# Top-k lists joined by more selection rounds, token numbers looked up in DRAM, and two operations moved to other engines

## The chip, the cores and the metric

The kernel runs on one core of a Trainium2 chip. The metric is device time in microseconds (us) of one execution. Five engines work in parallel: TensorE (PE in the profile) multiplies matrices, VectorE (DVE), ScalarE (ACT) and GpSimd (POOL) work on elements, SyncE (SP) issues transfers. Each takes its instructions strictly in order, and waits for the others by semaphores.

## What is computed

Attention over 8 batches, 12 heads, 448 tokens and head size 64, with q and k normalised by their root mean square; its output, as 3584 rows of 768, goes into a layer of 8 experts in which each expert takes at most 80 tokens, those with the largest gate weight:

```python
q_n, k_n = (rmsnorm(q, g_q), rmsnorm(k, g_k))
scores = scale * np.matmul(q_n, k_n.transpose(0, 1, 3, 2))
attn = softmax(scores)
x = np.matmul(attn, v)        # as rows of tokens: (3584, 768)
logits = x @ w_gate
expert_idx = np.argmax(logits, axis=1)
gate_w = softmax(logits)[np.arange(N), expert_idx]
for e in range(8):
    tok_idx = np.where(expert_idx == e)[0]
    if len(tok_idx) > 80:
        keep = np.argpartition(-gate_w[tok_idx], 80)[:80]
        tok_idx = tok_idx[keep]
    h = np.maximum(x[tok_idx] @ w1[e], 0.0)
    out[tok_idx] = gate_w[tok_idx, None] * (h @ w2[e])
```

## The kernel before, in words

The main loop (L447) runs n from -4 to 51. It is a software pipeline written out by hand: `ctx.enter_context(tc.manual_schedule())` makes every engine take the instructions in the order in which the loop writes them. Iteration n holds steps of several pairs of heads; there are 48 pairs, six to a batch. On TensorE an iteration computes the scores of pair n (L218), the product with v of pair n-1 (`av`, L228), the transposes of q and k of pair n+1 (L203), the gate sums of pairs n-3 and n-2 if n is odd (`zl`, L256 and L260), and the transposes that bring pair n-2 out (`xout`, L418). ScalarE squares q and k (L174), copies the transposed q and k out of PSUM (L208, L210), takes the exponential of the scores (L222) and copies `xout`'s result (L421). VectorE sums the exponentials over four tiles (`presum`, L237 to L239), sums the squares (`ssq`, L180), copies the product `po` out of PSUM (`uevac`, L244) and normalises q (L195, a = 0). GpSimd makes 1/sqrt of the mean square (L183, and the power at L186) and normalises k (L195, a = 1). `po` is a single PSUM buffer, so the product of the next pair waits for its copy. The buffers of tag `tp` in PSUM, two of them, serve every transpose.

When a batch's six pairs are through, `gate1`, `gate1t`, `gate1v` and `gate2` turn its sums into gate weights `S`, zero where an expert was not chosen, and `gate3` transposes them so that experts lie along partitions (`R`). Then comes the choice of the best 80. `rounds` takes them eight at a time: the eight largest values (MAX8), their positions (FIND_INDEX8) and a replacement of these by -2 (MATCH_REPLACE8), ten times. Batches 0 to 3 are done together, as 128 partitions of 448 columns; batches 4 to 6 one by one, as 128 partitions of 112 (each batch as four lists); batch 7 after the loop, 8 partitions of 448. `merge` joins two sorted lists with a bitonic network of eight stages: three comparisons on VectorE for the values, four operations on GpSimd that move the token numbers along. `bg` holds ten such merges in all. This work stands in `queue`; `work` takes pieces from it twice in an iteration, one piece while `slow` and three otherwise.

After the loop the rest of the queue runs, then the rounds of batch 7, a last join, and two transposes that give `idxT` (token numbers) and `gwT` (weights). Eight experts follow: a gather of 80 rows by indirect DMA (L544), two matrix products, a scatter into the output (L599). Weights of experts 0 to 3 are loaded during attention by GpSimd's queue, those of 4 to 7 are rewritten as bf16 in DRAM and loaded after the loop (L134).

Of the kernel before, what the change touches and what calls it, by code (L numbers as in the profile page):

```python
# [14 lines left out]
U32 = mybir.dt.uint32  # L15
PSUM = bass.MemoryType.PSUM
# [3 lines left out]
def kernel(  # L20
# [13 lines left out]
    nc = tc.nc  # L34
# [23 lines left out]

    cpool = ctx.enter_context(tc.tile_pool(name="const", bufs=1))
# [32 lines left out]


    LW = 128
    tpool = ctx.enter_context(tc.tile_pool(name="topk", bufs=1))
    lst = tpool.tile([128, 2, LW], F32, name="lst")
    other = tpool.tile([128, 2, LW], F32, name="other")
    ping = tpool.tile([128, 2, LW], F32, name="ping")
    pong = tpool.tile([128, 2, LW], F32, name="pong")
    best = tpool.tile([128, 2, LW], F32, name="best")  # L100
    for t in (lst, other):
        nc.gpsimd.memset(t[:, 0, :], -1.0)
        nc.gpsimd.memset(t[:, 1, :], 0.0)
# [41 lines left out]
    with tc.tile_pool(name="qk", bufs=3) as qkpool, \  # L145
# [148 lines left out]
        def gate2(b):  # L294
# [16 lines left out]

            if b < 4:
                if b == 0:
                    gst[0]["S"] = gpool.tile([ST, NT, 128], F32, tag="sc4", name="sc4", bufs=1)
                    nc.gpsimd.memset(gst[0]["S"][:], 0.0)
                dst = gst[0]["S"][:, :, 32 * b:32 * b + E]
            elif b < B - 1:
                gst[b]["S"] = gpool.tile([ST, NT, 32], F32, tag="sc1", name="sc1", bufs=1)
                nc.gpsimd.memset(gst[b]["S"][:], 0.0)
                dst = gst[b]["S"][:, :, 0:E]  # L320
            else:
                gst[b]["S"] = gpool.tile([ST, NT, E], F32, tag="sc7", name="sc7", bufs=1)
                dst = gst[b]["S"][:]
            nc.vector.tensor_mul(dst, eq[:], gw[:].unsqueeze(2).to_broadcast([ST, NT, E]))

        def gate3(b):

            if b < 3:
                return
            sp = tpps.tile([128, 512], F32, tag="tp", name="sp")  # L330
            if 3 < b < B - 1:
                nc.tensor.transpose(sp[:, :ST], gst[b]["S"][:].rearrange("p j c -> p (j c)"),
                                    ident[:ST, :ST])
                R = tpool.tile([128, ST], F32, tag="R1", name="R1")
                nc.vector.tensor_copy(R[:, :], sp[:, :ST])
            else:
                src = gst[0 if b == 3 else b]["S"]
                rows = src.shape[2]
                for j in range(NT):
                    nc.tensor.transpose(sp[:rows, j * ST:(j + 1) * ST], src[:, j, :],  # L340
                                        ident[:ST, :ST])
                R = tpool.tile([rows, S], F32, tag=f"R{rows}", name="R4")
                nc.vector.tensor_copy(R[:, :].rearrange("e (p j) -> e j p", j=NT),
                                      sp[:rows, :S].rearrange("e (j p) -> e j p", j=NT))
            gst[b]["R"] = R

        def rounds(b, step, off):

            rows = E if b == B - 1 else 128
            todo = []  # L350
            idx = tpool.tile([128, CAP], U32, tag="idx", name="idx", bufs=2)

            def one(kon):
                R = gst[b]["R"]
                mv = lst[:rows, 0, kon:kon + 8]
                nc.vector.max(out=mv, in_=R[:, :])
                nc.vector.max_index(out=idx[:rows, kon:kon + 8], in_max=mv, in_values=R[:, :])
                if kon + 8 < CAP:
                    nc.vector.match_replace(out=R[:, :], in_to_replace=mv,
                                            in_values=R[:, :], imm_value=-2.0)  # L360

            for kon in range(0, CAP, 8):
                todo.append(lambda kon=kon: one(kon))
            eng = nc.vector if b == B - 1 else nc.gpsimd
            last = todo[-1]

            def fin():
                last()
                eng.tensor_scalar(lst[:rows, 1, :CAP], idx[:rows, :], float(step),
                                  offq[:rows, off:off + 1], op0=ALU.mult, op1=ALU.add)  # L370
            todo[-1] = fin
            return todo

        def merge(a, pairs, res):


            todo = []

            def first():
                for dq, src, sq in pairs:  # L380
                    nc.gpsimd.tensor_copy(other[32 * dq:32 * dq + E, :, LW - CAP:],
                                          src[32 * sq:32 * sq + E, :, CAP - 1::-1])
                m = tpool.tile([128, LW], F32, tag="m0", name="m0")
                d = tpool.tile([128, LW], F32, tag="d0", name="d0")
                nc.vector.tensor_tensor(m[:, :], other[:, 0, :], a[:, 0, :], op=ALU.is_gt)
                nc.vector.tensor_tensor(ping[:, 0, :], other[:, 0, :], a[:, 0, :], op=ALU.max)
                nc.gpsimd.tensor_sub(d[:, :], other[:, 1, :], a[:, 1, :])
                nc.gpsimd.tensor_mul(d[:, :], d[:, :], m[:, :])
                nc.gpsimd.tensor_add(ping[:, 1, :], a[:, 1, :], d[:, :])

            def stage(i):
                w = LW >> (i + 1)
                x = (ping, pong)[i % 2]
                y = res if w == 1 else (pong, ping)[i % 2]

                def half(t, c, k):
                    return t[:, c, :].rearrange("p (g two w) -> p two g w", two=2, w=w)[:, k]
                m = tpool.tile([128, LW // w // 2, w], F32, tag="m1", name="m1", bufs=2)
                d = tpool.tile([128, LW // w // 2, w], F32, tag="d1", name="d1", bufs=2)
                va, vb, ua, ub = half(x, 0, 0), half(x, 0, 1), half(x, 1, 0), half(x, 1, 1)  # L400
                nc.vector.tensor_tensor(m[:], vb, va, op=ALU.is_gt)  # L401
                nc.vector.tensor_tensor(half(y, 0, 0), vb, va, op=ALU.max)
                nc.vector.tensor_tensor(half(y, 0, 1), vb, va, op=ALU.min)
                nc.gpsimd.tensor_sub(d[:], ub, ua)
                nc.gpsimd.tensor_mul(d[:], d[:], m[:])  # L405
                nc.gpsimd.tensor_add(half(y, 1, 0), ua, d[:])
                nc.gpsimd.tensor_sub(half(y, 1, 1), ub, d[:])

            todo.append(first)
            for i in range(7):  # L410
                todo.append(lambda i=i: stage(i))
            return todo
# [14 lines left out]
        def ok(n):  # L427
# [4 lines left out]
        bg[3] = (rounds(3, 1, 0)  # L432
                 + merge(lst, [(0, lst, 1), (2, lst, 3)], best)
                 + merge(best, [(0, best, 2)], best))
        for b in range(4, B - 1):
            bg[b] = (rounds(b, NT, 1 + b)
                     + merge(lst, [(0, lst, 1), (2, lst, 3)], lst)
                     + merge(lst, [(0, lst, 2)], lst)
                     + merge(best, [(0, lst, 0)], best))
        queue = []  # L440

        def work(k):
            for _ in range(k):
                if queue:
                    queue.pop(0)()

        for n in range(-4, NP + 4):  # L447
# [14 lines left out]
            for b in range(B):  # L462
# [3 lines left out]
                if n == b * HP + HP - 1 + 4 and b < B - 1:  # L466
# [11 lines left out]
            slow = len(queue) > 0 and n < 32  # L478
            work(1 if slow else 3)
# [11 lines left out]
            if ok(n + 3):  # L491
                rstd(n + 3)
# [4 lines left out]
            work(1 if slow else 3)  # L497
# [141 lines left out]
```

## Time and profile before

| | |
|---|---|
| median of 3 runs | 666.72 us (666.6 to 666.8) |
| the profiled execution, own time | 665.04 us |
| its span, first to last instruction | 663.1 us |
| mean granted clock of TensorE | 0.893 |
| busy: TensorE, VectorE, ScalarE, GpSimd | 514.8, 469.5, 300.7, 402.8 us |

Busy times are sums over one engine and run beside each other. Stretches with different limits follow one another, so the shares of the whole span say little; the rows further down are taken by stretch. An instruction in the trace stands with its start, its duration, its line, what it writes and reads, and in brackets the idle time of its engine just before it with what ended that.

### The profile page before, as it was taken

The numbers are of one execution on the slowest core, as the hardware profiler recorded it, in microseconds if no ns is written. First come the engines' busy times: TensorE is split into PE (matmuls) and PEld (weight loads), VectorE is DVE, ScalarE is ACT, GpSimd is POOL, SyncE is SP. The second block draws the span as 40 slices with busy tenths as digits, with TensorE's granted clock in tenths as the row PEclk, the third lists the DMA queues.
The fourth block names the chain that finished last, engine by engine and source line by source line (L and its number), as shares of the span: only waits on it lengthen the run. The fifth ranks groups of instructions, "written<-read, shape, count | busy, mean of one in ns | idle before, by whom it ended". The sixth has DMA issues, their size and how long they took to land. (4 is left out here: it accounts for less than half of the span.)

```text
span 663.1 us, 9227 instructions
## 1 busy us (share of the span) xinstructions
PE 514.8 (78%) x3101; PEld 221.4 (33%) x3101; DVE 469.5 (71%) x942; ACT 300.7 (45%) x409; POOL 402.8 (61%) x594
## 2 busy tenths in 40 slices
PE   0799999999999999998767976768867775000976
PEld 0334444434434334433222322222222321000854
DVE  1586677768778777999857875669756786786432
ACT  2667667666676676665433632343434330000111
POOL 2985445555544554452799696996997928843351
PEclk9999999999999999999888986887778797555989
DMA  3365969869788697794811834426416061541862
GB/s 98 115 137 151 249 151 261 172 179 240 176 237 177 189 254 155 230 199 142 175 49 58 161 92 93 101 70 132 117 28 125 14 125 28 209 173 30 297 235 60
DMA packets 82574, 97.55 MB, mean 147 GB/s; under 512 B 9056, under 2 KB 71008, under 8 KB 81504
## 3 DMA queue, kind: packets, MB, share of 16 engines
q1 hardware_dynamic: 66912, 67.85, 33.1%
q0 software_dynamic: 15616, 29.13, 24.8%
q8 instruction: 24, 0.39, 0.2%
q14 instruction: 22, 0.18, 0.1%
HBM read 97.97 MB, written 36.74 MB: 203 GB/s over the span
## 5 line engine op out<-in xcount | busy, mean ns | idle before, releaser
L228 PE MATMUL po<-at,vt 112*64 112x448 f32 x768 | 181.2, 597 | 45.0 <-DVE us L244 45.0
L222 ACT ACTIVATE at<-ps 112x896 f32<-112x896 f32 x192 | 165.9, 915 | 48.1 <-PE ps L218 42.3
L218 PE MATMUL ps<-qkT 64*112 64x448 f32 x768 | 176.5, 580 | 2.3 <-ACT qkT L210 1.3
L186 POOL TENSOR_TENSOR rs<-ms,nhalf 112x16 f32<-112x16 f32 x48 | 141.1, 2941 | 4.0
L183 POOL TENSOR_SCALAR ms<-ssq 112x16 f32<-112x16 f32 x48 | 11.4, 238 | 152.8 <-DVE ssq L180 151.7
L228 PEld LDWEIGHTS po<-at,vt 112*64 112x64 f32 x768 | 49.6, 144 | 162.1 <-issue 87.1
L218 PEld LDWEIGHTS ps<-qkT 64*112 64x112 f32 x768 | 62.9, 178 | 60.1 <-issue 37.1
L203 PE MATMUL tp<-ident,qn 112*128 112x112 f32 x384 | 52.9, 282 | 35.8 <-DVE qn L195 18.9
L238 DVE TENSOR_TENSOR t<-at 112x896 f32<-112x896 f32 x48 | 70.6, 1471 | 0.0
L203 PEld LDWEIGHTS tp<-ident,qn 112*128 112x128 f32 x384 | 40.6, 150 | 76.1 <-issue 35.7
L180 DVE TENSOR_REDUCE ssq<-sq 112x16 f32<-112x1024 f32 x48 | 58.1, 1210 | 9.6 <-ACT sq L174 9.6
L174 ACT ACTIVATE sq<-qk 112x1024 f32<-112x1024 f32 x48 | 50.6, 1055 | 30.3 <-DVE ssq L180 21.8
L208 ACT ACTIVATE qkT<-tp,gqk 128x448 f32<-128x448 f32 x48 | 30.2, 630 | 71.8 <-PE tp L203 71.5
L244 DVE COPY us<-po 128x448 f32<-128x448 f32 x48 | 29.6, 617 | 46.1 <-PE po L228 46.1
L195 POOL TENSOR_TENSOR qn<-qk,rs 112x512 f32<-112x512 f32 x48 | 58.7, 1224 | 2.1
L421 ACT COPY xb<-xp 112x512 f32<-112x512 f32 x48 | 28.2, 587 | 66.1 <-PE xp L418 66.1
L239 DVE TENSOR_TENSOR sm<-sm,t 112x896 f32<-112x896 f32 x48 | 54.1, 1126 | 1.6
L237 DVE TENSOR_TENSOR sm<-at 112x896 f32<-112x896 f32 x48 | 53.3, 1110 | 0.0
L195 DVE TENSOR_TENSOR qn<-qk,rs 112x512 f32<-112x512 f32 x48 | 37.8, 787 | 11.7 <-POOL rs L186 11.7
L580 ACT ACTIVATE h_sb<-ph 128x320 bf16<-128x320 f32 x16 | 7.0, 437 | 76.5 <-PE ph L576 76.5
L405 POOL TENSOR_TENSOR d<-d,m 128x64 f32<-128x64 f32 x77 | 32.5, 422 | 14.3 <-DVE m L401 8.5
L401 DVE TENSOR_TENSOR m<-ping 128x64 f32<-128x64 f32 x44 | 12.0, 272 | 35.2 <-POOL d L405 34.2
(114 smaller groups left out, 587.9 us busy)
## 6 DMA issues: line engine op xcount, KB each, us to landing
w_sb<-in_moe_w_dram POOLq DMA_DIRECT2D x8, 1536.0 KB, 15.6
wb_scratch<-in_moe_w_dram POOLq DMA_DIRECT2D x8, 1536.0 KB, 11.8
w_sb<-wb_scratch SPq DMA_DIRECT2D x8, 1536.0 KB, 11.6
qk<-in_q_dram SPq DMA_DIRECT2D x48, 224.0 KB, 4.3
qk<-in_k_dram SPq DMA_DIRECT2D x48, 224.0 KB, 4.5
vt<-in_v_dram SPq DMA_DIRECT2D x48, 224.0 KB, 4.7
xr_scratch<-xb SPq DMA_DIRECT2D x48, 224.0 KB, 3.4
out_dram<-zeros SPq DMA_DIRECT2D x28, 384.0 KB, 6.6
```

The lines of the kernel that those rows point to most:

```text
L174: nc.scalar.activation(sq[:, :], st[n]["qk"][:].rearrange("p a h x -> p (a h x)"), AF.Square)
L180: nc.vector.reduce_sum(out=ssq[:, :], in_=st[n]["sq"][:].rearrange("p (g d) -> p g d", d=D), axis=AX.X)
L186: nc.gpsimd.tensor_tensor(rs[:].rearrange("p a h j -> p (a h j)"), ms[:, :], nhalf[:, :], op=ALU.pow)
L195: eng.tensor_mul(qn[:, a].rearrange("p j h d -> p h j d"), qk[:, a].rearrange("p h (j d) -> p h j d", d=D), rs[:, a].unsqueeze(3).to_broad ...
L203: nc.tensor.transpose(tp[:, j * ST:(j + 1) * ST], st[n]["qn"][:, a, j].rearrange("p h d -> p (h d)"), ident[:ST, :ST])
L218: nc.tensor.matmul(ps[:, hh, :S], st[n]["T1"][hh * D:(hh + 1) * D, j * ST:(j + 1) * ST], st[n]["T0"][hh * D:(hh + 1) * D, :], start=True, ...
L222: nc.scalar.activation(st[n]["at%d" % (j // 2)][:, j % 2], ps[:, :, :S], AF.Exp)
L228: nc.tensor.matmul(st[n]["po"][hh * D:(hh + 1) * D, :S], st[n]["v"][:, hh, j * D:(j + 1) * D], st[n]["at%d" % (j // 2)][:, j % 2, hh, :], ...
L237: nc.vector.tensor_add(sm[:], a0[:, 0], a0[:, 1])
L238: nc.vector.tensor_add(t1[:], a1[:, 0], a1[:, 1])
L239: nc.vector.tensor_add(sm[:], sm[:], t1[:])
L405: nc.gpsimd.tensor_mul(d[:], d[:], m[:])
```

## The change

There are no merges any more. The 80 best of batches 0 to 3 are taken as before; then `lists` adds each batch's first token number to the positions, stores these token numbers in a DRAM table `tab_scratch` (four transfers on SP's queue) and copies the four lists of values side by side into one row of 320 columns per expert (`cand["a"]`, GpSimd). Ten further rounds over these 320 columns give the best 80 of the four batches. Batches 4 and 5 are treated together in the same way (64 partitions of 448 columns), and joined with the 80 so far in ten rounds over 240 columns; batch 6 is written beside the 80 so far and joined in ten rounds over 528. Each of these joins ends in positions, not in token numbers. `numbers` turns positions into addresses of the table (`place`: GpSimd adds, TensorE transposes, VectorE casts), fetches the numbers with eight indirect DMAs on GpSimd's queue, one for each expert, 80 words each, and stores them for the next level (SP). Batch 7 is joined after the loop as before, with three transposes.

`work` now spends a budget of 4.2 (in us as the code reckons them) once, at an iteration's end, instead of counting pieces. `uevac` copies on ScalarE; both halves of `normalise` are on GpSimd; `rstd` stands behind `uevac`. The work of the queue is spread as follows: rounds of batches 0 to 3 in iterations 27 to 30, their join in 30 to 33, lookups in 33 and 34; rounds of batches 4 and 5 in 39 to 42, the join in 42 to 44, lookups in 45; the join with batch 6 in 46 to 50, lookups in 51.

```diff
+    LT = CAP + S
+    tab_dram = nc.dram_tensor("tab_scratch", (E, 3, LT), U32, kind="Internal").ap()
...
-            eng = (nc.vector, nc.gpsimd)[a]
-            eng.tensor_mul(
+            nc.gpsimd.tensor_mul(
...
-            nc.vector.tensor_copy(us[:, :], st[n]["po"][:, :S])
+            nc.scalar.copy(us[:, :], st[n]["po"][:, :S])
...
+            first, rows = {3: (0, 128), 5: (4, 64)}.get(b, (b, E))
...
+        def rounds(get, rows, width, val):
+            idx = tpool.tile([rows, CAP], U32, tag="idx", name="idx", bufs=2)
+            def one(kon):
+                R, v = get(), val[:, kon:kon + 8]
+                nc.vector.max(out=v, in_=R)
+                nc.vector.max_index(out=idx[:, kon:kon + 8], in_max=v, in_values=R)
                 if kon + 8 < CAP:
+                    nc.vector.match_replace(out=R, in_to_replace=v, in_values=R, imm_value=-2.0)
+            cost = (3 * (width + 60) / 960 + 0.3, )
+            return [cost + (lambda kon=kon: one(kon), ) for kon in range(0, CAP, 8)], idx
+        def lists(b0, nb, val, idx, lev, dst, col):
+            def go():
+                num = tpool.tile([32 * nb, CAP], U32, tag="num", name="num")
+                nc.gpsimd.tensor_scalar(num[:, :], idx[:, :],
+                                        offq[:32 * nb, b0 // 4:b0 // 4 + 1], None, op0=ALU.add)
+                for g in range(nb):
+                    nc.sync.dma_start(out=tab_dram[:, lev, col + g * CAP:col + (g + 1) * CAP],
+                                      in_=num[32 * g:32 * g + E, :])
+                    nc.gpsimd.tensor_copy(dst[:, col + g * CAP:col + (g + 1) * CAP],
+                                          val[32 * g:32 * g + E, :])
+            return [(0.0, go)]
+        def numbers(idx, lev, res):
+            add = tpool.tile([CAP, E], U32, tag="add", name="add")
+            def place():
+                pf = tpool.tile([E, CAP], F32, tag="pf", name="pf")
+                nc.gpsimd.tensor_scalar(pf[:, :], idx[:, :], tabF[:, :], float(lev * LT),
+                                        op0=ALU.add, op1=ALU.add)
+                tp = tpps.tile([128, 512], F32, tag="tp", name="tpn")
+                nc.tensor.transpose(tp[:CAP, :E], pf[:, :], ident[:E, :E])
+                nc.vector.tensor_copy(add[:, :], tp[:CAP, :E])
+            def fetch(e):
+                nc.gpsimd.indirect_dma_start(
+                    out=res[:, e:e + 1], out_offset=None,
+                    in_=tab_dram.rearrange("e l (s o) -> (e l s) o", o=1),
+                    in_offset=bass.IndirectOffsetOnAxis(ap=add[:, e:e + 1], axis=0))
+            def store():
+                if lev < 2:
+                    nc.sync.dma_start(out=tab_dram[:, lev + 1, :CAP].rearrange("e s -> s e"),
+                                      in_=res[:, :])
+            return ([(0.3, place)] + [(0.5, lambda e=e: fetch(e)) for e in range(E)]
+                    + [(0.0, store)])
-        def merge(a, pairs, res):
...
+        r, i = rounds(lambda: gst[3]["R"], 128, S, v03)
+        bg[3] = r + lists(0, 4, v03, i, 0, cand["a"], 0)
+        r, i = rounds(lambda: cand["a"][:, :], E, 4 * CAP, cand["b"])
+        bg[3] += r + numbers(i, 0, num3)
+        r, i = rounds(lambda: gst[5]["R"], 64, S, v45)
+        bg[5] = r + lists(4, 2, v45, i, 1, cand["b"], CAP)
+        r, i = rounds(lambda: cand["b"][:, :], E, 3 * CAP, cand["c"])
+        bg[5] += r + numbers(i, 1, num5)
+        r, i = rounds(lambda: cand["c"][:, :], E, LT, best)
+        bg[6] = r + numbers(i, 2, num6)
...
+        def work(us):
+            while queue and us > 0:
+                cost, f = queue.pop(0)
+                f()
+                us -= cost
...
-            slow = len(queue) > 0 and n < 32
-            work(1 if slow else 3)
...
-            work(1 if slow else 3)
...
+            work(4.2)
```

What the order of instructions becomes shows best in three places. The first is VectorE in an iteration that takes rounds over batches 0 to 3; before, from one `us` copy to the next (`R_2413` holds the gate weights, `lst` the lists):

```order
L244 COPY us<-po 128x448 [waits PE_49]
L356 MAX lst<-R_2413 128x8 [waits DVE_49]
L357 MAX_INDEX idx<-lst,R_2413 128x8 [waits DVE_49]
L359 MATCH_REPLACE R_2413<-lst,R_2413 128x448 [waits DVE_49]
L237 TENSOR_TENSOR sm<-at 112x896
L238 TENSOR_TENSOR t_2524<-at 112x896 [waits Activation_49]
L239 TENSOR_TENSOR sm<-sm,t_2524 112x896 [waits DVE_49]
L356 MAX lst<-R_2413 128x8
L357 MAX_INDEX idx<-lst,R_2413 128x8 [waits DVE_49]
L359 MATCH_REPLACE R_2413<-lst,R_2413 128x448 [waits DVE_49]
L195 TENSOR_TENSOR qn<-qk,rs 112x2x4x64 [waits DMAHW3_49,Pool_49]
L180 TENSOR_REDUCE ssq<-sq 112x16 [waits Activation_49]
```

And VectorE with the change at the end of iteration 30 and the start of 31, where the last round over single batches stands before the first over the joined row:

```order
L187 TENSOR_REDUCE ssq<-sq 112x16 [waits Activation_49,Pool_49]
L349 MAX v_154<-R 128x8
L350 MAX_INDEX idx<-v_154,R 128x8 [waits DVE_49]
L349 MAX candb<-canda 8x8 [waits Pool_49]
L350 MAX_INDEX idx<-candb,canda 8x8 [waits DVE_49]
L352 MATCH_REPLACE canda<-candb,canda 8x320 [waits DVE_49]
L349 MAX candb<-canda 8x8 [waits DVE_49]
L350 MAX_INDEX idx<-candb,canda 8x8 [waits DVE_49]
L352 MATCH_REPLACE canda<-candb,canda 8x320 [waits DVE_49]
L243 TENSOR_TENSOR sm<-at 112x896 [waits PE_49]
L244 TENSOR_TENSOR t_2781<-at 112x896 [waits Activation_49]
```

The copy of `po` and one `qn` are gone from VectorE, all rounds of an iteration stand behind `ssq`, and the first round over `canda` waits for GpSimd. The second place is GpSimd in iterations 33 and 34 with the change (lines L190 to L201 are the old L183 to L195, `num_157` the token numbers):

```order
L201 TENSOR_TENSOR qn<-qk,rs 112x2x4x64 [waits DMAHW2_49,PE_49,Pool_49]
L201 TENSOR_TENSOR qn<-qk,rs 112x2x4x64 [waits DMAHW3_49]
L190 TENSOR_SCALAR ms<-ssq 112x16 [waits DVE_49]
L193 TENSOR_TENSOR rs<-ms,nhalf 112x16 [waits Pool_49]
L376 TENSOR_SCALAR pf<-idx,tabF 8x80 [waits DVE_49]
L383 DMA num_157<-tab_scratch,add 80x1 [waits DMAHW1_49,DMAHW6_49,DMAHW0_49,DMAHW7_49,DMASW3_49,DVE_49]
L383 DMA num_157<-tab_scratch,add 80x1 [waits DMASW4_49]
L201 TENSOR_TENSOR qn<-qk,rs 112x2x4x64 [waits DMAHW7_49,PE_49,Pool_49]
L201 TENSOR_TENSOR qn<-qk,rs 112x2x4x64 [waits DMAHW0_49]
L190 TENSOR_SCALAR ms<-ssq 112x16 [waits DVE_49]
L193 TENSOR_TENSOR rs<-ms,nhalf 112x16 [waits Pool_49]
L383 DMA num_157<-tab_scratch,add 80x1 [waits DMASW5_49]
```

Two lookups stand ahead of the `qn` of iteration 34, and six more behind its power. The third place is TensorE at the end of iteration 33, with the change:

```order
L234 MATMUL po<-at,vt 64x448 x4
L399 MATMUL xp<-ident,us 112x128 [waits Activation_49]
L399 MATMUL xp<-ident,us 112x128 x3
L379 MATMUL tpn<-ident,pf 80x8 [waits Activation_49,Pool_49]
L224 MATMUL ps<-qkT 112x448 [waits Activation_49]
```

The transpose of `pf` stands ahead of the scores of the next iteration, and waits for GpSimd, which waits for the last round on VectorE.

## Rows read from the trace of the kernel before

**Rows 1.** The page's slices: busy tenths of TensorE and its granted clock

```profile
PE   0799999999999999998767976768867775000976
PEclk9999999999999999999888986887778797555989
```

**Rows 2.** Busy us (and instructions) of each engine by stretch, clock, DMA share, GB/s

```profile
core 0: us, PE busy (x) PEld busy (x) DVE busy (x) ACT busy (x) POOL busy (x), PEclk, DMA share, GB/s
100.00:120.00 20.00, 20.00 (x118) 7.93 (x116) 15.64 (x16) 13.69 (x19) 13.49 (x10) 1.00 0.80 218
...
400.00:420.00 20.00, 11.99 (x57) 4.82 (x57) 13.85 (x38) 7.14 (x10) 13.96 (x32) 0.79 0.62 126
...
580.00:600.00 20.00, 0.00 (x0) 0.00 (x0) 16.76 (x47) 0.00 (x0) 7.09 (x22) 0.50 0.35 149
```

**Rows 3.** TensorE in order of time: the first scores of four iterations

```profile
99.45 1.76 PE L218 MATMUL ps<-qkT 64*112 64x448 f32 x8
...
109.28 1.76 PE L218 MATMUL ps<-qkT 64*112 64x448 f32 x8
...
117.47 1.76 PE L218 MATMUL ps<-qkT 64*112 64x448 f32 x8
...
273.15 1.76 PE L218 MATMUL ps<-qkT 64*112 64x448 f32 x8
```

**Rows 4.** TensorE in order of time: a wait for VectorE's copy

```profile
327.80 3.26 PE L228 MATMUL po<-at,vt 112*64 112x448 f32 x8 [3.91 <-DVE us L244]
```

**Rows 5.** VectorE in order of time: first and last of batch 7, addresses

```profile
584.69 0.61 DVE L356 MAX8 lst<-R 8x8 f32<-8x448 f32 x1
...
604.75 0.25 DVE L369 TENSOR_SCALAR lst<-idx,offq 8x80 f32<-8x80 uint32 x1
...
606.73 0.16 DVE L536 CAST idxT<-ft 80x8 uint32<-80x8 f32 x1 [0.46 <-PE ft L533]
```

**Rows 6.** VectorE in order of time: the adds of `presum`, and `ssq`

```profile
37.42 1.08 DVE L237 TENSOR_TENSOR sm<-at 112x896 f32<-112x896 f32 x1
...
40.55 2.24 DVE L195 TENSOR_TENSOR qn<-qk,rs 112x512 f32<-112x512 f32 x1
...
302.56 1.21 DVE L180 TENSOR_REDUCE ssq<-sq 112x16 f32<-112x1024 f32 x1
303.69 0.61 DVE L244 COPY us<-po 128x448 f32<-128x448 f32 x1
```

**Rows 7.** VectorE in order of time: one round over 112 columns

```profile
541.55 0.27 DVE L356 MAX8 lst<-R 128x8 f32<-128x112 f32 x1
...
542.61 0.28 DVE L356 MAX8 lst<-R 128x8 f32<-128x112 f32 x1
```

**Rows 8.** GpSimd in order of time: root mean square and `qn`, list copies

```profile
303.86 0.21 POOL L183 TENSOR_SCALAR ms<-ssq 112x16 f32<-112x16 f32 x1 [5.88 <-DVE ssq L180]
304.15 2.90 POOL L186 TENSOR_TENSOR rs<-ms,nhalf 112x16 f32<-112x16 f32 x1
307.12 1.06 POOL L195 TENSOR_TENSOR qn<-qk,rs 112x512 f32<-112x512 f32 x1
...
546.31 0.66 POOL L381 COPY other<-lst 8x160 f32<-8x160 f32 x2
```

**Rows 9.** VectorE in order of time: a gate, from its first operation to the next `presum`

```profile
316.22 0.44 DVE L280 RECIPROCAL rz<-zt 112x48 f32<-112x48 f32 x1
...
319.81 1.08 DVE L237 TENSOR_TENSOR sm<-at 112x896 f32<-112x896 f32 x1
```

**Rows 10.** Groups of instructions and DMA issues: gathers, small pieces, us to landing

```profile
L544 POOL DMA_INDIRECT xg<-xr_scratch,idxT x8 | 8.3, 1036 | 21.4 <-issue 19.5 <-POOL xg L543 1.9
...
xr_scratch<-rz SPq DMA_DIRECT2D x8, 21.0 KB, 7.5
```

**Rows 11.** VectorE in order of time: an add beside GpSimd's normalisation

```profile
118.54 2.82 DVE L238 TENSOR_TENSOR t<-at 112x896 f32<-112x896 f32 x1
```

**Rows 12.** Instructions on `R`: duration ns min/median/max, first and last start us

```profile
L356 DVE MAX8 lst<-R x50: 260/278/621, 267.6 to 603.4; 128x8 f32<-128x112 f32 x30, 128x8 f32<-128x448 f32 x10, 8x8 f32<-8x448 f32 x10
...
L343 DVE COPY R<-sp x2: 927/938/948, 263.7 to 578.5; 128x448 f32<-128x448 f32 x1, 8x448 f32<-8x448 f32 x1
```

More of the change, by code (lines that the diff above doesn't have):

```diff
@@ L324, in gate2 @@
[L324 to L344, printed above, removed]
+            first, rows = (0, 128) if b < 4 else (4, 64) if b < 6 else (b, E)
@@ new lines, in gate2, with gate3 @@
+            if b == first:
+                gst[b]["S"] = gpool.tile([ST, NT, rows], F32, tag=f"sc{rows}", name="sc", bufs=1)
+                if rows > E:
+                    nc.gpsimd.memset(gst[b]["S"][:], 0.0)
+            r0 = 32 * (b - first)
+            nc.vector.tensor_mul(gst[first]["S"][:, :, r0:r0 + E], eq[:],
+                                 gw[:].unsqueeze(2).to_broadcast([ST, NT, E]))
+        def gate3(b):
+            if b not in (3, 5, 6, 7):
+                return
+            first, rows = {3: (0, 128), 5: (4, 64)}.get(b, (b, E))
+            sp = tpps.tile([128, 512], F32, tag="tp", name="sp")
+            for j in range(NT):
+                nc.tensor.transpose(sp[:rows, j * ST:(j + 1) * ST], gst[first]["S"][:, j, :],
+                                    ident[:ST, :ST])
+            if b == 6:
+                R = cand["c"][:, CAP:]
+            else:
+                R = tpool.tile([rows, S], F32, tag=f"R{rows}", name="R")[:, :]
+            nc.vector.tensor_copy(R.rearrange("e (p j) -> e j p", j=NT),
+                                  sp[:rows, :S].rearrange("e (j p) -> e j p", j=NT))
@@ L358, in one @@
                 if kon + 8 < CAP:
[L359 to L370, printed above, removed]
@@ L371, in rounds @@
-            todo[-1] = fin
-            return todo
-        def merge(a, pairs, res):
[L377 to L412, printed above, removed]
@@ L431 @@
         bg = {}
[L432 to L439, printed above, removed]
-        queue = []
[L442 to L445, printed above, removed]
+        v03 = tpool.tile([128, CAP], F32, name="v03")
+        v45 = tpool.tile([64, CAP], F32, name="v45")
+        best = tpool.tile([E, CAP], F32, name="best")
+        num3 = tpool.tile([CAP, E], U32, name="num3")
+        num5 = tpool.tile([CAP, E], U32, name="num5")
+        num6 = tpool.tile([CAP, E], U32, name="num6")
+        r, i = rounds(lambda: gst[3]["R"], 128, S, v03)
[8 more added lines that the diff above has]
+        bg[6] = r + numbers(i, 2, num6)
+        queue = []
+        def work(us):
[3 more added lines that the diff above has]
+                us -= cost
         for n in range(-4, NP + 4):
@@ L504 @@
                     gate3(b)
+            work(4.2)
+        while queue:
+            work(1)
     wlate = ctx.enter_context(tc.tile_pool(name="moe_w2", bufs=1))
@@ L511 @@
         fetch_late(e)
-    while queue:
-        work(1)
-    for f in rounds(B - 1, 1, B):
-        f()
-    fin = tpool.tile([E, 2, CAP], F32, name="fin")
-    fm = tpool.tile([E, CAP], F32, name="fm")
-    fd = tpool.tile([E, CAP], F32, name="fd")
-    A, Z = best[:E, :, :CAP], lst[:E, :, CAP - 1::-1]
-    nc.vector.tensor_tensor(fm[:, :], Z[:, 0], A[:, 0], op=ALU.is_gt)
-    nc.vector.tensor_sub(fd[:, :], Z[:, 1], A[:, 1])
-    nc.vector.tensor_mul(fd[:, :], fd[:, :], fm[:, :])
-    nc.vector.tensor_tensor(fin[:, 0], Z[:, 0], A[:, 0], op=ALU.max)
@@ L536 @@
-    nc.vector.tensor_copy(idxT[:, :], ft[:CAP, E:2 * E])
-    nc.vector.tensor_copy(gwT[:, :], ft[:CAP, 0:E])
+    v7 = tpool.tile([E, CAP], F32, name="v7")
+    last, lidx = rounds(lambda: gst[B - 1]["R"], E, S, v7)
+    for cost, f in last:
+        f()
+    fin = tpool.tile([E, 3, CAP], F32, name="fin")
+    nc.vector.tensor_tensor(fin[:, 0], v7[:, ::-1], best[:, :], op=ALU.is_gt)
+    nc.vector.tensor_tensor(fin[:, 1], v7[:, ::-1], best[:, :], op=ALU.max)
+    nc.vector.tensor_scalar(fin[:, 2], lidx[:, ::-1], float((B - 1) * S), None, op0=ALU.add)
@@ new lines @@
+    ft = tpps.tile([128, 512], F32, tag="tp", name="ft")
+    for i in range(3):
+        nc.tensor.transpose(ft[:CAP, i * E:(i + 1) * E], fin[:, i], ident[:E, :E])
+    old = tpool.tile([CAP, E], F32, name="old")
+    new = tpool.tile([CAP, E], F32, name="new")
+    gwT = tpool.tile([CAP, E], F32, name="gwT")
+    bad = tpool.tile([CAP, E], F32, name="bad")
+    idxT = tpool.tile([CAP, E], U32, name="idxT")
+    nc.vector.tensor_copy(old[:, :], num6[:, :])
+    nc.vector.tensor_sub(new[:, :], ft[:CAP, 2 * E:3 * E], old[:, :])
```

65 lines of the change are left out of this document (22 added, 43 removed).

## The prediction

> **What bounds the kernel now.** I read the slices of the page first, then the busy times by stretch, then each engine in order of time. Two slice rows [rows 1] give the shape: TensorE is full for 17 slices of 16.6 us, then falls to 6 to 8 tenths for most of the next sixteen, to nothing for three, and fills again for the experts; its granted clock follows it down. From 400 to 420 us TensorE works 12.0 us of 20 at a mean clock of 0.79, and VectorE and GpSimd 14 us each; from 580 to 600 TensorE does nothing, VectorE 16.8 us [rows 2]. So three stages have three limits.
>
> In the first, TensorE sets the pace: an odd iteration (with the `zl` matmuls) takes 109.28 - 99.45 = 9.83 us, the even one behind it 8.19 [rows 3]. Iteration 28 starts at 273.15, so iteration 27, where list work starts, at T = 273.15 - 9.83 = 263.3. From there TensorE waits for the `us` copy on VectorE, which stands in VectorE's queue behind list work: at 327.8 it waits 3.91 us, and the eight matmuls behind that take 3.26 us where eight of the same size take about 1.7 in [rows 3], which is the lower clock level [rows 4]. Merge stages on VectorE in turn wait for GpSimd's half. The last stage is ten rounds of batch 7 from 584.69 to 604.75 and some arithmetic; addresses are ready at 606.89, and the span ends at 663.1 [rows 5]. Those last 56.3 us are the experts, which the change does not touch.
>
> **What VectorE pays per iteration.** The three adds of `presum` take 40.55 - 37.42 = 3.13 us when nothing disturbs them, and `ssq` 303.69 - 302.56 = 1.13 [rows 6]. The `us` copy and `qn` leave, so 4.26 us stay. A round over 448 columns costs 2.07 (20.06 for ten, the last without its replace [rows 5]), one over 112 columns 542.61 - 541.55 = 1.06 [rows 7], though it has 128 partitions and the other eight: width counts. On that line 240 columns cost 1.44, 320 cost 1.69 and 528 cost 2.31.
>
> **Removed and moved.** Ten merges of eight stages leave VectorE and GpSimd, and with them the wait of TensorE for `us`: ScalarE now copies `po`. ScalarE is busy 13.7 us of 20 in the first stage [rows 2], 6.2 per 9 us iteration; a copy like VectorE's at some 0.6 fits, and I cost it at nothing. Its cover is gone only where ScalarE waits in `gate2` for VectorE, an instant that the VectorE sum below holds already. GpSimd does both `qn`: `ms`, pow and one `qn` take 307.12 - 303.86 + 1.06 = 4.3 us [rows 8], two 5.4, under 8.19. `transp` reads them more than an iteration later, so only the start pays, one `qn` or **1 us**.
>
> **First lists, iterations 27 to 33.** I follow VectorE from the end of `ssq` in iteration 27, T + 6 (some 5 us after the scores start, and 1 for adds that meet a `qn`). `work(4.2)` takes three rounds of 448 in each of 27 to 29: 6.2, then twice 4.26 + 6.2, to T + 33.1. In 30 comes the tenth round, and the next `MAX` waits for GpSimd's copies, which stand behind `ms` and pow: 3.3 us after `ssq`, then five small operations at 0.33 [rows 8], 5.0 in all; with two rounds of 320 (3.4) and 4.26 it is 12.7. Iteration 31 has the `zsb` copy (0.55) and three rounds, 9.9; iteration 32 a gate, 319.81 - 316.22 = 3.6 us [rows 9], and three rounds, 12.9; iteration 33 two rounds and `place`, which goes to GpSimd, TensorE and back (four short operations, 0.9), 8.5. That ends at T + 77.1. TensorE's own work in these seven is 4 x 9.83 + 3 x 8.19 + 0.6 for `zt` = 64.5. Its transpose in `place` must wait for VectorE, so **12.6 us** are lost there at the latest, and I add 3 for a spell at the lower clock [rows 4]. Iterations 34 to 38 have no rounds; TensorE paces them, 45.2 us with a `zt` and an `sp`. Iteration 39 starts at T' = T + 125.3.
>
> **Second and third lists, 39 to 51.** The same from T' + 6: 6.2 and twice 10.46, to T' + 33.1; iteration 42 is 4.26 + 4.3 for the wait and two rounds of 240, 11.5; 43 is 10.6; 44 has a gate, the copy into the candidates (0.95 [rows 12]) and four rounds, 14.6; 45 is 3.3. That is T' + 73.1, which TensorE's 64.9 lie inside. Iterations 46 to 48 are 3.13 + 2 x 2.31 each, 49 is 5.2, 50 is 9.1 (gate, copy of batch 7, last two rounds), `place` 0.9: T' + 111.6. Ten rounds of 448 and the closing arithmetic, about the 606.89 - 584.69 = 22.2 of today [rows 5], end at T' + 133.8; experts to **T' + 190.1**.
>
> **Lookups.** An indirect DMA holds GpSimd 1.04 us [rows 10], so eight after the first lists are 8.3 us. They delay the next `qn`, which has some 11 us before `transp` needs it; the eight at the end run beside batch 7's 20 us. I cost them at nothing at 1.04 each. The other bound is that each holds GpSimd until its words land: 7.5 us, as the small pieces of `rz` take [rows 10]; the row for an indirect DMA is the nearer one, the bound is rival (d). SP's six list stores and two stores of looked-up numbers wait ahead of later loads. Those run an iteration ahead, so I take zero, and 5 us as the upper end at each of three waits.
>
> **Sum.** 263.3 + 1.0 + 125.3 + 190.1 = 579.7 us of span. Around the span of the profiled execution lie 665.04 - 663.1 = 1.9, and the median of the runs is 1.7 above that execution: **583 us**.
>
> **The port, row against rule.** Beside GpSimd's `qn` an add of `presum` took 2.82 us [rows 11], against 1.08 undisturbed [rows 6]; no `MAX8` takes over 0.621 [rows 12]. In iterations with rounds the two `qn` begin 3.3 us after `ssq`, under the rounds, so I charge nothing beyond the 1 us above. The Trainium skill (SBUF — State Buffer, Who interferes with whom) says that a VectorE instruction with two SBUF inputs and a GpSimd instruction that reads SBUF shut each other out for a whole instruction, and that one with a single input does not contend. By that rule, the rows agree; it speaks against moving `qn`, and is the first rival.
>
> **Rivals.** (a) The moved `qn` falls on the adds after all. Then each of 13 iterations that VectorE paces and that still have a `qn` costs 2.82 - 1.08 = 1.7 more, 22 us: 605. For it: rows 11; against: the order above. (b) VectorE's lag is absorbed by buffers and TensorE alone paces: iterations 27 to 47 are 192.6 us, two short ones 7, gate and copy of batch 7 some 5, then the 22.2 and 56.3 of above; with 263.3 + 1 + 3.6 that is 551. Against: `place` puts TensorE behind VectorE twice. (c) Small costs add up: SP's waits hold back q and k, TensorE drops to the lower level more often; 15 to 25 us, around 603. (d) Slower than before: each lookup holds GpSimd until it lands. With a hold of h, the first eight cost 8h less 11.5 of cover, the second 8h less 39 (until the third lists need GpSimd), the third 8h less 22. At 1.0 + 7.5 that is 24 x 8.5 - 72.5 = 131, so 714 us; from h = 6.5 on it eats the whole gain of 84. Against: 1.04 in the row. (e) The wait removed was not the limit and another takes its place: near 665.
>
> **How the numbers follow.** Forecast (569 to 595) 0.62, (a) 0.14, (b) 0.08, (c) 0.11, (d) 0.03, (e) 0.02. The range 564 to 614 takes in the forecast, (a) and (c) with the SP waits, 0.87 nominally; I leave the rest for terms that no row shows. A measurement of this kernel tells 0.2% (1.3 us) from no change; faster by more 0.95, same 0.01, slower 0.04.
>
> **What would show it.** Right: TensorE full until the first lists, then waiting at the transpose of `place` and at `zt`, never for `us` on VectorE; iteration 39 near 390 us; batch 7's ten rounds beginning near 501; no merge groups; experts still 56 us. Wrong: `presum` adds that take over 3.5 us together where rounds run (a), GpSimd standing between lookups (d), long waits of `sq` for q or k (c).

## The result, and the profile after

The changed kernel takes **595.18 us** (median of four runs, 594.05 to 595.29) against 666.66 us (666.27 to 666.8) on the same chip: a ratio of 0.8925, 95% interval 0.8909 to 0.894. That is 71.5 us less; the forecast was 84 less, 583 us, and its range (564 to 614) holds the result. It lies at the upper edge of the forecast's own band (569 to 595), in the part of the range that was left for rivals and SP's waits. The profiled execution has a span of 593.3 us.

The slices of its page, TensorE and its granted clock, answer to [rows 1]:

```profile
PE   0699999999999999999987699399997995005795
PEclk9999999999999999999997979699997998556998
```

A slice is 14.8 us here. The long stretch of 6 to 8 tenths is gone. What is left of it are a dip around 320 us, a hole from 370 to 385 (the 3), and two empty slices ahead of the experts where there were three of 16.6 us. The groups of instructions show the moves (busy us, mean ns of one, then idle time just before them):

```profile
L234 PE MATMUL po<-at,vt 112*64 112x448 f32 x768 | 168.2, 560 | 0.1
...
L201 POOL TENSOR_TENSOR qn<-qk,rs 112x512 f32<-112x512 f32 x96 | 112.2, 1196 | 2.7
...
L181 ACT ACTIVATE sq<-qk 112x1024 f32<-112x1024 f32 x48 | 50.7, 1057 | 27.2 <-DMA qk<-in_k_dram 24.6 <-DVE ssq L187 2.6
...
L383 POOL DMA_INDIRECT num<-tab_scratch,add x24 | 26.9, 1121 | 8.9 <-issue 5.7 <-DVE add L380 2.6 <-DMA w_sb<-wb_scratch 0.3
...
L250 ACT COPY us<-po 128x448 f32<-128x448 f32 x48 | 25.7, 534 | 25.4 <-PE po L234 24.7 <-issue 0.7
```

The matmuls into `po` no longer wait for the `us` copy (0.1 us in all; at one place alone it was 3.91 [rows 4]). A copy on ScalarE costs 0.53, a lookup about 1.1. What has grown is on `sq`: ScalarE waits 24.6 us for `k` from DRAM, 11.58 of them at once. Before it was 7.3, beside longer waits for `ssq`:

```profile
L174 ACT ACTIVATE sq<-qk 112x1024 f32<-112x1024 f32 x48 | 50.6, 1055 | 30.3 <-DVE ssq L180 21.8 <-DMA qk<-in_k_dram 7.3 <-DVE sm L239 1.2
```

TensorE in order of time, its long waits from iteration 27 to the experts:

```profile
314.46 1.07 PE L278 MATMUL zt<-ident,zsb 128*112 128x128 f32 x4 [4.24 <-ACT xb L402]
...
341.86 0.23 PE L379 MATMUL tpn<-ident,pf 8*80 8x8 f32 x1 [5.88 <-POOL pf L376]
342.02 3.33 PE L224 MATMUL ps<-qkT 64*112 64x448 f32 x8
...
379.80 1.10 PE L399 MATMUL xp<-ident,us 128*112 128x128 f32 x4 [8.77 <-ACT qkT L214]
...
401.87 1.76 PE L224 MATMUL ps<-qkT 64*112 64x448 f32 x8
...
451.34 1.07 PE L278 MATMUL zt<-ident,zsb 128*112 128x128 f32 x4 [3.17 <-ACT xb L402]
...
506.26 0.91 PE L333 MATMUL sp<-ident,sc 112*8 112x112 f32 x4 [7.31 <-DVE sc L323]
...
512.59 0.23 PE L379 MATMUL tpn<-ident,pf 8*80 8x8 f32 x1 [5.42 <-POOL pf L376]
...
533.33 0.40 PE L515 MATMUL ft<-ident,fin 8*80 8x8 f32 x3 [20.50 <-DVE fin L511]
```

All but one are where the prediction put them: at `zt`, at the transpose of `place`, at `sp` behind the gate of iteration 50, which its sum has on VectorE, and in the last rounds. The one that it lacks is the largest before the last batch: 8.77 us at 379.80, for `qkT`. Iteration 39 starts at 401.87; the forecast is T' = 389.6, so 12.3 us of the shortfall lie before it. What stands behind that wait is read on three engines. ScalarE:

```profile
378.17 1.06 ACT L181 ACTIVATE sq<-qk 112x1024 f32<-112x1024 f32 x1 [11.58 <-DMA qk<-in_k_dram]
379.13 0.62 ACT L214 ACTIVATE qkT<-tp,gqk 128x448 f32<-128x448 f32 x1
```

`sq` waits 11.58 us for `k`, and the `qkT` copy for TensorE stands behind it. SP's queue of DMA issues:

```profile
353.64 0.56 SPq L403 DMA_DIRECT2D xr_scratch<-xb  x1
361.35 0.31 SPq L390 DMA_DIRECT2D tab_scratch<-num  x1
361.76 0.46 SPq L166 DMA_DIRECT2D qk<-in_q_dram  x1
362.27 0.68 SPq L168 DMA_DIRECT2D qk<-in_k_dram  x1
```

The loads of `q` and `k` stand behind the store of token numbers, which waits for the lookups; those run on GpSimd from 342.57 to 359.9 and have a weight rewrite right behind them:

```profile
358.98 0.90 POOL L383 DMA_INDIRECT num<-tab_scratch,add  x1 [0.30 <-issue]
359.89 0.96 POOL L136 DMA_DIRECT2D wb_scratch<-in_moe_w_dram  x1
```

So three things meet at 360 us: loads that SP holds back, a store of 640 single words ahead of them (2.5 KB, 16.1 us from issue to landing), and 1.5 MB from DRAM to DRAM beside them:

```profile
tab_scratch<-num SPq DMA_DIRECT2D x1, 2.5 KB, 16.1
```

The experiments take these apart.

### The profile page after: what moved, and what is told of

Same layout as the page of the kernel before. It is cut to its first block, busy times and chain, and to the rows that moved or that the text cites. A ratio compares the mean times of both kernels' runs of the same rounds, so it can differ in the third digit from the quotient of the medians.

```text
span 593.3 us, 8594 instructions
## 1 busy us (share of the span) xinstructions
PE 496.1 (84%) x3110; PEld 217.9 (37%) x3110; DVE 379.5 (64%) x644; ACT 322.3 (54%) x457; POOL 354.4 (60%) x285
## 2 busy tenths in 40 slices
DMA packets 84761, 97.55 MB, mean 164 GB/s; under 512 B 11240, under 2 KB 73200, under 8 KB 83696
## 5 line engine op out<-in xcount | busy, mean ns | idle before, releaser
L234 PE MATMUL po<-at,vt 112*64 112x448 f32 x768 | 168.2, 560 | 0.1
L190 POOL TENSOR_SCALAR ms<-ssq 112x16 f32<-112x16 f32 x48 | 26.8, 557 | 150.7 <-DVE ssq L187 149.8
L201 POOL TENSOR_TENSOR qn<-qk,rs 112x512 f32<-112x512 f32 x96 | 112.2, 1196 | 2.7
L244 DVE TENSOR_TENSOR t<-at 112x896 f32<-112x896 f32 x48 | 53.0, 1105 | 30.4 <-ACT at L228 30.3
L209 PE MATMUL tp<-ident,qn 112*128 112x112 f32 x384 | 49.4, 272 | 20.0 <-POOL qn L201 19.3
L181 ACT ACTIVATE sq<-qk 112x1024 f32<-112x1024 f32 x48 | 50.7, 1057 | 27.2 <-DMA qk<-in_k_dram 24.6
L245 DVE TENSOR_TENSOR sm<-sm,t 112x896 f32<-112x896 f32 x48 | 59.0, 1228 | 1.6
L572 ACT ACTIVATE h_sb<-ph 128x320 bf16<-128x320 f32 x16 | 6.9, 437 | 72.8 <-PE ph L568 72.8
L250 ACT COPY us<-po 128x448 f32<-128x448 f32 x48 | 25.7, 534 | 25.4 <-PE po L234 24.7
L399 PE MATMUL xp<-ident,us 128*112 128x128 f32 x192 | 31.6, 288 | 8.8 <-ACT qkT L214 8.8
L399 PEld LDWEIGHTS xp<-ident,us 128*112 128x112 f32 x192 | 19.7, 135 | 42.7 <-ACT at L228 24.7
L383 POOL DMA_INDIRECT num<-tab_scratch,add x24 | 26.9, 1121 | 8.9 <-issue 5.7
```

The lines of the kernel that those rows point to most:

```text
L181: nc.scalar.activation(sq[:, :], st[n]["qk"][:].rearrange("p a h x -> p (a h x)"), AF.Square)
L201: nc.gpsimd.tensor_mul(qn[:, a].rearrange("p j h d -> p h j d"), qk[:, a].rearrange("p h (j d) -> p h j d", d=D), rs[:, a].unsqueeze(3).to ...
L209: nc.tensor.transpose(tp[:, j * ST:(j + 1) * ST], st[n]["qn"][:, a, j].rearrange("p h d -> p (h d)"), ident[:ST, :ST])
L234: nc.tensor.matmul(st[n]["po"][hh * D:(hh + 1) * D, :S], st[n]["v"][:, hh, j * D:(j + 1) * D], st[n]["at%d" % (j // 2)][:, j % 2, hh, :], ...
L244: nc.vector.tensor_add(t1[:], a1[:, 0], a1[:, 1])
L245: nc.vector.tensor_add(sm[:], sm[:], t1[:])
```

## Experiments

Every kernel was timed in three rounds against the kernel before on the same chip, which gave 667.5, 667.3 and 666.8 us in the three sets. Edits are against the changed kernel (595.18 us) unless said otherwise.

**The store one iteration later.**

```diff
+            wait = [(4.2, lambda: None)] * (1 if lev == 0 else 0)
             return ([(0.3, place)] + [(0.5, lambda e=e: fetch(e)) for e in range(E)]
-                    + [(0.0, store)])
+                    + wait + [(0.0, store)])
```

> Base: the changed kernel, 595.2 us. In its trace TensorE stands still 8.8 us at 371 to 380 us because the square of pair 39 waits 11.6 us for k. Edit: the store of the first looked-up numbers goes one iteration later on SP, behind the loads of pair 39 and with the lookups landed by then; it still meets the weight rewrite of 1.5 MB. Theory hold (SP stood in front of the store until the lookups landed, 7 us, and the loads with it): the wait is gone, 583 to 587 us. Theory clog (the store is 640 pieces of one word and takes 16 us on the DMA engines beside the rewrite, and loads queued behind it arrive late whenever it is issued): the wait moves to the loads of pair 40, 592 to 597 us.

Measured: **583.36 us**, ratio 0.8743 (0.8728 to 0.8757). SP's queue in its trace:

```profile
354.46 0.57 SPq L166 DMA_DIRECT2D qk<-in_q_dram  x1
...
365.78 0.37 SPq L390 DMA_DIRECT2D tab_scratch<-num  x1
366.26 1.20 SPq L166 DMA_DIRECT2D qk<-in_q_dram  x1
```

The loads that were held until 361.76 now leave at 354.46, and no wait of TensorE over 0.3 us is left between 342 and 410. The place of one store of 2.5 KB is worth 11.8 us. The loads behind the words are still late: ScalarE waits 4.84 us for `k` of the next pair at 379.10. TensorE has the time.

**The store three iterations later.** The same edit with 3 for 1.

> Edit: the same store three iterations later, when no weight rewrite is in flight and the lookups have long landed. Hold: 583 to 587 us, as with one iteration. Clog by the words alone: 592 to 597 us, a wait of k for a later pair of 8 us or more. Clog only together with the rewrite: 583 to 588 us here, but 592 or more with one iteration's delay.

Measured: 590.14 us (0.8809 to 0.8858). Later is not better, and none of the three expected outcomes holds, since the moment is not the one that was meant: the store falls at the end of iteration 37 (382.51), 1.3 us behind another rewrite (381.18), and the wait comes back: ScalarE waits 7.87 us for `k` at 400.62 and TensorE 3.02 at 402.26. So a held queue is not needed; words with a rewrite beside them do it too.

**Two rounds of work per iteration ahead of iteration 39, not three.**

```diff
-            work(4.2)
+            work(2.9 if n < 39 else 4.2)
```

> Edit: the budget of work is 2.9 in place of 4.2 up to iteration 38, so that the first lists take two rounds per iteration over iterations 27 to 36. My theory of the forecast (TensorE loses 12 us there because VectorE has 10.5 us of work per iteration against TensorE's 9, and pays at zt and at the transpose of place): the 4.2 us wait at zt and the 5.9 us wait at place shrink to under 2 each and the spells at the lower clock behind them go, 12 to 15 us less: 580 to 584 us, if the store's wait stays. Rival (the time is TensorE's wait for GpSimd's chain, whatever VectorE's load): place still waits over 4 us, 590 to 595.

Measured: **580.16 us**, ratio 0.869 (0.8676 to 0.8705). The waits at `zt` (4.24) and `place` (5.88) of the first lists are gone; the largest there is 2.54. But a wait of the same kind comes further on. SP is held until 392.50, and the words stand ahead of the loads; a rewrite issued at 380.20 has started its last packet by 391.2, and the words land in 7.6 us, so no rewrite is needed beside them:

```profile
404.71 1.10 PE L399 MATMUL xp<-ident,us 128*112 128x128 f32 x4 [6.31 <-ACT qkT L214]
```

**Both: two rounds, and the store one iteration later.**

> Two edits of earlier runs together: two rounds per iteration before iteration 39 instead of three, and the store of token numbers one iteration after the last lookups. Alone they gave 580.2 and 583.4. Theory 'two separate waits': the spread one keeps a wait of 6.3 us for qkT and its spell at the lower clock, some 8 us, which the later store takes away: 572 (568 to 577), and no wait of TensorE over 3 us in iterations 27 to 42. Rival 'the same slack counted twice' (what TensorE no longer waits for there, it waits for at the second lists): 579 or more.

Measured: **572.75 us** (571.41 to 574.31), ratio 0.8588 (0.8561 to 0.8616). The two waits are separate. It beats both kernels: 22 us under the changed one, 94 under the one before. The slices of its page are

```profile
PE   0599999999999999999999889999997994005895
PEclk9999999999999999999999999989998999556999
```

with no slice under 8 tenths between the first two and some 425 us. TensorE's largest waits in iterations 27 to 42 are 2.52 and 2.29 us.

**Rows instead of words.** The store writes eight rows of 320 bytes, positions instead of token numbers.

```diff
-                    nc.sync.dma_start(out=tab_dram[:, lev + 1, :CAP].rearrange("e s -> s e"),
-                                      in_=res[:, :])
+                    nc.sync.dma_start(out=tab_dram[:, lev + 1, :CAP], in_=idx[:, :])
```

> Edit: both stores write the positions, eight rows of 320 bytes that need no lookup, in place of the looked-up numbers, 640 single words. Left out: the token numbers of the earlier levels, so rows of x are gathered by position. Both theories: no wait of k, 582 to 587 us; this is the whole price of the store. If the wait stays (592 or more), neither theory holds and the rewrite of weights or the lookups themselves delay the loads.

Measured: 588.17 us (0.8796 to 0.8826). The store still overwrites a table that the lookups read, so SP issues it at 362.31, as late as before. TensorE waits 4.29 us for `qkT` instead of 8.77, ScalarE 7.10 for `k`. The words are about half of it, and the time lies between what was expected with the wait and without it. (The profiled execution took 592.77 us, the other four 588.1 to 589.2, so the waits are of the longest one.) The page counts the words: packets under 512 bytes fall from 11240 to 9960, by 1280, or 640 for each of the two stores. The Trainium skill (DMA: Bandwidth & Descriptors, Rules for kernel authors) says that an access whose last dimension isn't contiguous is cut into one descriptor per element; the count agrees.

**The rewrite one iteration earlier.** It goes to the stretch in which the DMA engines moved nothing (348 to 352 us).

```diff
-            if n >= 2 and n % 3 == 2 and NW0 <= n // 6 < E:
-                stage_w(n // 6, n % 6 // 3)
+            m = {34: 35, 35: 34}.get(n, n)
+            if m >= 2 and m % 3 == 2 and NW0 <= m // 6 < E:
+                stage_w(m // 6, m % 6 // 3)
```

> The changed kernel with one weight rewrite (1.5 MB from DRAM to DRAM on GpSimd's queue) put into iteration 34, where the DMA engines moved nothing from 344 to 352 us, instead of iteration 35, where it was issued right behind the lookups at 359.9. The store of token numbers stays where it was, so SP still holds the loads of pair 39 until about 361. Theory 'SP's hold and the small words are enough': the wait of 8.8 us stays at 5 us or more and the time is 590 to 596. Rival 'the loads come late because they share the queues with the rewrite': the wait falls under 2.5 us and the time is 584 to 588.

Measured: 589.33 us (0.8814 to 0.885), TensorE's wait 5.36 us. By the wait the first theory holds, by the time neither, since it lies between their ranges. With the rewrite away, the words are seen alone, in the busy times by stretch (last three columns: granted clock, DMA share, GB/s):

```profile
364.00:368.00 4.00, 4.00 (x26) 1.71 (x22) 1.57 (x2) 1.10 (x2) 3.92 (x2) 1.00 0.78 29
368.00:372.00 4.00, 1.71 (x10) 0.47 (x8) 0.00 (x0) 0.00 (x0) 2.44 (x3) 1.00 0.71 56
372.00:376.00 4.00, 0.93 (x4) 0.69 (x4) 1.40 (x2) 2.56 (x4) 0.09 (x1) 0.69 1.09 305
```

For 8 us the DMA engines are over seven tenths busy at 29 and 56 GB/s, with loads of 224 KB waiting behind; then these come at 305. The store takes 7.8 us to land, against 16.1 beside the rewrite. The packets that the trace records say more: beside the rewrite, words start in the same number as the rewrite's packets of 1536 bytes (252 of each from 366 to 368 us in the changed kernel); alone, nearly all words have started by 366, and what follows are slow packets of the loads, 95 in the next 2 us where the run below has 484 from 364 on.

**Rows, and the rewrite earlier.** Both edits; SP stays held.

> The changed kernel with both edits that shortened the wait of 8.8 us by about half each: the store writes eight rows of positions (which leaves out the token numbers of the first lists), and the weight rewrite moves to iteration 34. SP is still held until the lookups are done, some 362 us. Theory 'the hold only makes the loads late; it is the small words and the rewrite, in the queue with them, that make them too late': no wait of TensorE over 1.5 us near 375, and 582 to 586. Rival 'a load issued at 362 is too late whatever else moves': a wait of 4 us or more remains and the time is 587 to 590.

Measured: 580.12 us (577.99 to 584.1), ratio 0.8714 (0.8668 to 0.876). SP issues store and loads at 362.20 to 362.96, as late as ever, and TensorE runs through. ScalarE's wait for `k`:

```profile
366.35 1.06 ACT L181 ACTIVATE sq<-qk 112x1024 f32<-112x1024 f32 x1 [1.87 <-DMA qk<-in_k_dram]
```

This closes the square: waits of 8.77 us (words and rewrite), 4.29 (rewrite alone), 5.36 (words alone), none near 375 (neither); times 595.2, 588.2, 589.3, 580.1. The hold by itself costs nothing here; it uses up the lead that the loads had, and what shares the queues with them then decides. The time came out 2 us under what was expected.

**The copy of `po` back on VectorE.**

```diff
-            nc.scalar.copy(us[:, :], st[n]["po"][:, :S])
+            nc.vector.tensor_copy(us[:, :], st[n]["po"][:, :S])
```

> The changed kernel with the copy of po back on VectorE, in its old place. Theory 'the copy on ScalarE cuts TensorE loose from VectorE': with it back, each of some 16 iterations with rounds goes at VectorE's pace of 4.3 + 0.55 + 6.2 = 11 us instead of only catching up at zt and at the place transpose; TensorE waits 15 us or more for us in all, and the time is 605 to 625. Rival 'the shorter list alone does it': within 4 us of 595.

Measured: **624.27 us** (0.9336 to 0.9379 of before; 29 us lost), as the first theory had it, but not by its waits. TensorE's matmuls into `po` still wait 0.1 us in all. It is VectorE that waits, since `us` stands ahead of `ssq` and the rounds, for TensorE to finish:

```profile
274.19 0.62 DVE L250 COPY us<-po 128x448 f32<-128x448 f32 x1 [3.25 <-PE po L234]
274.73 1.21 DVE L187 TENSOR_REDUCE ssq<-sq 112x16 f32<-112x1024 f32 x1
275.85 0.62 DVE L349 MAX8 v<-R 128x8 f32<-128x448 f32 x1
...
282.07 1.08 DVE L243 TENSOR_TENSOR sm<-at 112x896 f32<-112x896 f32 x1
```

The first rounds start at 275.85 instead of 270.94, and an iteration with rounds then takes VectorE 11.0 us instead of 10.5, so that `place` comes 8.1 us later (349.95). The lag then grows at each further list, and TensorE's wait at `qkT` to 9.98 us.

**One normalisation of two back on VectorE.** `nc.gpsimd` becomes `(nc.vector, nc.gpsimd)[a]` at `qn`.

> The changed kernel with one normalisation of two back on VectorE. It costs VectorE 1.2 us in each iteration, and stands behind ms and pow of GpSimd, some 3.5 us after ssq. Theory 'VectorE sets the end of the first and second lists, so its terms count one for one': 7 and 6 iterations of 1.2 us, half of the second inside TensorE's own pace, and some 5 at the third lists: 15 to 22 us, 608 to 617. Rival 'VectorE has slack there': within 4 us of 595.

Measured: 601.88 us (0.8966 to 0.9039), 6.7 lost. Both theories missed. The trace has the cause:

```profile
279.56 0.69 DVE L201 TENSOR_TENSOR qn<-qk,rs 112x512 f32<-112x512 f32 x1
280.16 1.21 DVE L187 TENSOR_REDUCE ssq<-sq 112x16 f32<-112x1024 f32 x1
```

VectorE does in 0.69 us, with 0.60 to the next start, what takes GpSimd 1.2 in the mean, so the price put on it was nearly twice too high; and it stands ahead of `ssq`, so its `rs` is of the iteration before and seldom waited for. `place` comes only 2.1 us later (344.00); the wait for `qkT` grows to 11.43 us.

**Both back: the new lists alone.**

> The new lists with neither move: copy of po and one normalisation on VectorE, as in the kernel before. The moves alone gave 668.0, the copy put back gave 624.3. Theory 'the parts add on VectorE': 29 us for the copy and some 15 for the normalisation on top of 595, 635 to 645, so the lists alone are worth some 27 us and the moves are worth 45 only with them. Rival 'either edit put back already ties TensorE to VectorE, the second adds little': 622 to 630.

Measured: 630.01 us (0.9392 to 0.9462), at the edge of the rival's range. Its number holds, its reason does not: put back alone the copy costs 29.1 us and the normalisation 6.7, together 34.8, so the two very nearly add. What was wrong in the first theory is the 15 us for the normalisation.

**The two moves alone**, in the kernel before:

```diff
-            eng = (nc.vector, nc.gpsimd)[a]
-            eng.tensor_mul(
+            nc.gpsimd.tensor_mul(
...
-            nc.vector.tensor_copy(us[:, :], st[n]["po"][:, :S])
+            nc.scalar.copy(us[:, :], st[n]["po"][:, :S])
```

> The kernel before with only the two moves (copy of po on ScalarE, both normalisations on GpSimd); its merges stay. Theory 'the new list is most of the gain, the moves only let it show': the 45 us that TensorE waits for us on VectorE turn largely into waits at zt and for gate results, and merges wait for a GpSimd that has 1.2 us more per iteration: 645 to 667. Rival 'the moves are most of the gain': 625 or less.

Measured: 667.97 us, ratio 1.0012 (0.9997 to 1.0026): no difference. The wait for `us` is gone, 0.8 us in all instead of many like [rows 4]. TensorE waits for what VectorE and GpSimd do in its place:

```profile
397.26 0.60 PE L202 MATMUL tp<-ident,qn 112*128 112x112 f32 x4 [2.07 <-POOL qn L194]
406.28 0.98 PE L202 MATMUL tp<-ident,qn 112*128 112x112 f32 x4 [8.42 <-DVE lx L283]
424.25 0.98 PE L202 MATMUL tp<-ident,qn 112*128 112x112 f32 x4 [5.46 <-POOL d L403]
```

So the new lists alone, with the way in which `work` now deals them out, are worth 36.7 us (666.7 to 630.0), the moves alone nothing, and both 71.5: half the gain comes from having them together. No run takes the lists and the dealing apart. The time is 1 us over what was expected.

## Why the prediction was right, and where it was short

**The start, right but for a term.** Iteration 27 starts at 263.18; the forecast is 263.3 and 1.0 for the prologue. That 1.0 is not there: in the iterations that TensorE paces, neither move costs anything.

**VectorE sets the first and third lists: right.** `place` of the first lists comes 341.86 - 263.18 = 78.7 us after T (forecast 77.1), behind the wait of 3.60 for GpSimd's copies that the sum had (3.3). The 1.6 are there from the first round, which starts 7.8 us after T (270.94) where the sum has 6: `sq` waits 2.63 us for `k` at 268.64. A round over 448 columns starts every 2.1 us. The edit of `work` confirms the mechanism: with fewer rounds per iteration the waits at `zt` and `place` go.

**Iterations 34 to 38: the step that failed.** From `place` to iteration 39 the kernel takes 401.87 - 341.86 = 60.0 us; the forecast is 45.2 and 3 for the lower clock, 48.2. "Those run an iteration ahead, so I take zero": this is the term, SP's stores at nothing. The runs show 11.8 us at this one store (the first edit), against an upper end of 5. With the store moved, `place` to iteration 39 takes 390.60 - 341.78 = 48.8 us, so the other terms of the 48.2 were right. The mechanism was named in rival (c), "SP's waits hold back q and k, TensorE drops to the lower level more often", but at some 20 us for three places; it struck at one, with the sign given for it, a long wait of `sq` for `k`. The upper end was sized by the hold alone. What was left out is that the store is 640 words, ahead of the loads, and that GpSimd's lookups push a rewrite into the same moment. Behind the wait of 8.77 comes a spell at the lower level, as at 342.02, where eight matmuls take 3.33 us instead of 1.76 (granted clock 0.50, the level of 1.2 GHz, from 376 to 384):

```profile
380.00:384.00 4.00, 3.86 (x12) 1.57 (x11) 3.68 (x4) 3.62 (x6) 3.28 (x2) 0.50 0.18 50
```

**From iteration 39 on: right.** 593.3 - 401.87 = 191.4 us, forecast 190.1. VectorE is through with the second lists at 474.69, 72.8 us after iteration 39 (forecast 73.1). The third `place` comes 110.7 us after iteration 39 (forecast 111.6), addresses are ready 22.2 us behind it (534.8), as in [rows 5], and from there to the end are 58.5 us, forecast 56.3. The experts, taken as untouched, cost 2.2 more, and 0.9 less at `place` hides a part of it.

In sum the span missed by 13.6 us: 1.1 less at the start, 1.6, 11.8 and 1.3 more. The median stands 1.9 above the span here, where the forecast carried 3.6 over from before. The 1.7 less around the span and the 1.1 at the start hide a part of the miss, which is 12.2 us in the median; that is luck.

**The copy on ScalarE at nothing: right.** Its 25.7 us do not delay iteration 27, and TensorE waits for it 0.1 us in all. The reason given, a TensorE that no longer waits for `us`, was only half of it: the run with the copy put back lost 29 us on VectorE's side of that tie.

**Rival (a), the port: refuted here.** In nearly all iterations with rounds the adds are as undisturbed as in [rows 6]:

```profile
277.16 1.08 DVE L243 TENSOR_TENSOR sm<-at 112x896 f32<-112x896 f32 x1
278.16 1.08 DVE L244 TENSOR_TENSOR t<-at 112x896 f32<-112x896 f32 x1
279.28 1.09 DVE L245 TENSOR_TENSOR sm<-sm,t 112x896 f32<-112x896 f32 x1
```

Three adds from iteration 27 on took 1.82 us (266.20, 335.02, 404.88), 2.2 us more in all, where the rival has 22.

**Rival (b), absorption: no.** TensorE waits at every `place` but the second. **Rival (d), lookups that hold GpSimd: no.** Six in a row start 1.2 us apart (352.85 to 358.98), where the rival has 8.5. **Rival (e): no**, though the moves without the lists behave just so.

## What to carry to other kernels

That a store is of a few kilobytes does not make it free: count its contiguous pieces, look at which loads stand behind it on its queue, and at what else starts in that moment. Give such a store a place where its data has been ready for an iteration, and where no large transfer begins. Of two changes one can be worth nothing alone and half the gain beside the other, where the work that remains ties the engines to each other; so a part is priced with the others in place. Work dealt out to an engine should fit into the pace of the engine that it must not hold up: two rounds per iteration instead of three were worth 15 us, more than the store.

## What the hardware showed that was not expected

640 words of four bytes took 7.6 and 7.8 us to land with no rewrite beside them, 16.1 with 1.5 MB from DRAM to DRAM beside them, and the loads queued behind came late with them. A normalisation over 112 x 512 takes VectorE 0.69 us and GpSimd 1.2 in the mean. Most lookups held GpSimd for 0.9 to 1.0 us, but three of the changed kernel's 24 for 2.3 to 2.7: the first behind `place` at 342.57 and 474.98, and the sixth at 482.78. The first of the third lists took 1.01 (513.31), and with two rounds per iteration the first of all took 1.07, so this isn't a property of the first, and its cause stays open.
